# Filler matmuls in the idle stretches of a planned attention and MoE kernel, with a plan tuned anew

## The chip, the cores and the metric

The kernel runs on one core of one Trainium2 chip. The metric is the device time of one execution in microseconds (us); the number compared is the median of several runs. The engines are PE (matrix products), DVE (vector), ACT (scalar functions), POOL (the general-purpose engine) and SP, which issues most transfers.

## What is computed

Attention keeps only the 32 largest scores of each row, and its output feeds a two-layer network with the gate h * tanh(softplus(h)). Everything is float32 in effect; the two weight matrices arrive as float64.

```python
q, k, v: (4, 8, 576, 64)          # batch, heads, sequence, head width
w_in: (512, 2048), w_out: (2048, 512)
scores = q @ k.T / sqrt(64)
kth = the 32nd largest score of each row
attn = softmax(where(scores >= kth, scores, -1e9))
x = (attn @ v) as (2304, 512)     # the 8 heads side by side
h = x @ w_in
sp = where(h > 20, h, log1p(exp(min(h, 20))))
out = (h * tanh(sp)) @ w_out      # (2304, 512)
```

## The kernel before, in words

**A planner writes the order.** The kernel does not issue its work in loops. `build` describes every operation to a `Plan`: its engine, an estimated duration, what it depends on, which ring buffers it takes and frees, and a priority. `Plan.schedule` then plays the work through: again and again it takes, over all engines, the operation that could start earliest by its estimates, and at equal starts the one with the smaller priority number. The resulting start times fix the order of the instructions on each engine's queue; on the chip each queue runs in order and waits by semaphores. So durations and priorities change nothing that is computed, only the order. Some operations name a second way on another engine (`also`); the planner takes the way that ends first, with a penalty for the second way (BIAS).

**Attention.** A unit is one batch, one pair of heads and one tile of 128 query rows (the last tile of a sequence has 64 rows and both heads share one slot). A full unit has two slots, one per head; there are 144 slots. Per slot: PE transposes the queries and multiplies them with the keys (line 638), ACT copies the 576 scores out of PSUM (line 655), DVE finds the 24 largest (lines 670 to 684: eight maxima of eight chunks, then maxima and replacements). How many scores lie below the 24th largest is counted either by DVE (line 703) or by ACT with a sign function (line 699): the share CSH decides. POOL multiplies the mask into the scores (line 707), DVE takes the next eight maxima (line 713), which yields the threshold. The exponential and the masking are then done by ACT and DVE (lines 756 and 758) or, for a share MSH, by ACT and POOL (lines 748 to 752). PE transposes the weights (line 803), ACT copies them (line 809), PE multiplies them with the values (line 839), and DVE writes the normalized rows to xr (lines 855 and 858).

**Weights.** Both matrices are loaded in 16 pieces each of 512 KB (line 422) into staging buffers (pools STG and STX), and float64 is turned into float32 by bit operations: POOL shifts the low word (line 428), ACT scales the high word into PSUM (line 435), DVE joins them (line 445). The sign is put in by DVE (line 441) or, for a share SGN ("apart"), by an ACT sign pass (line 439) and a POOL product (line 450). Except for the first six pieces of the second matrix, each piece is split into a high and a low part for the matrix engine; the low part is a subtraction on POOL (line 476) or, for a share PLO, an identity product and a subtracting product on PE (lines 469 and 470) with a copy on ACT (line 473). While pieces are being prepared, six of the eight hidden-layer buffers serve as staging; `release` gives them back when the last piece is done.

**The network.** The 2304 tokens form 9 groups of 256. A group can start when all eight heads of its tokens are in xr; it is split into high and low parts (lines 906 to 917). The first layer is 16 blocks of 12 matmuls (line 940), the nonlinearity runs on ACT in batches (lines 952 to 972), POOL or DVE multiply and split (lines 987 to 1000), and the second layer accumulates 16 blocks in the two banks psO (lines 1009 and 1013) until `flush` copies them out and stores them. The planner's pool "O" has one entry: it is taken by a group's first block of the second layer and given back by the flush.

**Priorities.** Attention work has the slot's number plus an offset OFF[0..8, 11..] by kind (OFF[0] for loads of keys and queries, one less than that or more by a few), weight pieces WPR[0] + WPR[1] * i (+ WPO for the second matrix), group g of the network MLP0 + MLPS * 16 * g + LAG[g].

**The matrix engine's clock in the plan.** The planner counts the columns that PE streams in steps of TICK us; if the step before an operation had fewer than WARM, it plans the operation at twice its duration.

The planner's durations for DVE are linear in the length: `dve(n)` is (1.0417 n + 72) ns, `held(n, extra)` the same plus extra, for operations that exclude POOL in the plan.

Of the kernel before, what the change touches and what calls it, by code (L numbers as in the profile page):

```python
# [33 lines left out]
             TB=2, HB=8, GH=2, GL=3, XS=1, OB=1, C=2)  # L34
FIFO = ("S", "Y", "C", "M8", "SM", "WT", "WX", "RB", "KN", "KS", "QN", "QS", "QL", "V")
XR = 512
MLP0 = 58.83975636082121
MLPS = 1.121860262315038
LAG = (-25.995810819941177, -26.474079155792758, -19.13806320546605, -18.854128398230255, -7.786063767408372, -8.799346239468274, -12.371711128172647, -1.6692882578445132, -7.591562462708602)
OFF = (-16.98515120479643, 2.328093500794843, -3.96944656014681, 3.035426527996102, 0.4828418529158596, 0.7164642923464081, -1.649352757422735, 0.6592529327519733, -28.765739384772523, -3.5228328815861154, 6.763792071250068, -2.9083787972029063, 9.183328578610238)  # L40
WPO = -0.6274142379880567
CSH = [(18, 0.8667247802625605), (999, 0.3323003066774938)]
MSH = [(11, 0.919392917195224), (999, 0.13298644690001551)]
WPR = (19.149617763081373, 0.047652472774268644)
DELTA = 0
ALSO = True
N2 = 6
LOCK = True
TAB = 1.4
BIAS = [(48.89001834786856, 12.94226098178285), (724.1096866960131, 0.9005748864757063), (1000000000.0, 0.29275323803529374)]  # L50
PLO = [(16, 0.7434170351780047), (999, 0.21870871979825823)]
SGN = 0.3679529210622342
PH = {3: ([0, 1], [2], [3, 4])}

SLACK = {'pe': 0.2487527268649277, 'dve': 0.0, 'act': 0.0, 'pool': 0.3014222492564422}
TICK = 3.413
WARM = 3060

# [24 lines left out]
class Plan:  # L85
# [7 lines left out]
    def __init__(self, sizes):  # L93
        self.sizes = sizes
        self.ops = []
        self.slot = {}

    def op(self, eng, dur, fn, deps=(), alloc=(), free=(), prio=0.0, cols=0, also=(), tab=None):

# [8 lines left out]
    def schedule(self):  # L108
        free = {p: [(0.0, i) for i in range(n)] for p, n in self.sizes.items()}
        turn = {p: [] for p in FIFO}  # L110
        for o in self.ops:
            o.left = len(o.deps)
            for d in o.deps:
                d.users.append(o)
            for p in {p for p, _ in o.alloc}:
                if p in turn:
                    turn[p].append(o)
        for p in turn:
            turn[p].reverse()
        avail = {e: 0.6 if e == "sp" else 2.3 for o in self.ops for e, _, _ in o.ways}  # L120
        moved = 0.0
        port = {"pool": 0.0, "dve": 0.0}
        cand = [(o, [0.0] * len(o.ways)) for o in self.ops if o.left == 0]
        ndone = 0
        order = []
        ticks = {}

        loaded, window, left = "exp", None, 0

        def pool_ready(o):  # L130
            need = {}
            for p, _ in o.alloc:
                need[p] = need.get(p, 0) + 1
                if p in turn and turn[p][-1] is not o:
                    return None
            r = 0.0
            for p, n in need.items():
                if len(free[p]) < n:
                    return None
                r = max(r, sorted(free[p])[n - 1][0])  # L140
            return r

        while ndone < len(self.ops):
            best = {}
            for c in cand:
                o, rs = c
                if o.tab and window and (o.tab == "exp" or o.tab[1] != window):
                    continue
                pr = pool_ready(o) if o.alloc else 0.0
                if pr is None:  # L150
                    continue
                w = None
                for x, (e, d, _) in enumerate(o.ways):
                    load = TAB if o.tab and (o.tab == "exp") != (loaded == "exp") else 0.0
                    st = max(avail[e] + load, rs[x], pr)
                    if LOCK and e == "pool":
                        st = max(st, port["dve"])
                    elif LOCK and isinstance(d, Held):
                        st = max(st, port["pool"])
                    fin = st + d + (next(b for t, b in BIAS if st < t) if x else 0.0)  # L160
                    if w is None or fin < w[0]:
                        w = (fin, st, x)
                e = o.ways[w[2]][0]
                best.setdefault(e, []).append((w[1], o.prio, o.seq, w[2], c))
            if not best:
                stuck = sorted({(o.prio, o.eng, tuple(p for p, _ in o.alloc)) for o, _ in cand})
                raise RuntimeError(f"no operation can go on: {stuck[:12]}")
            pick = None
            for e, lst in best.items():
                lo = min(x[0] for x in lst) + DELTA  # L170
                x = min((y for y in lst if y[0] <= lo), key=lambda y: (y[1], y[2]) if DELTA else (y[0], y[1], y[2]))
                if pick is None or x[:3] < pick[:3]:
                    pick = x
            s, _, _, x, c = pick
            o = c[0]
            cand.remove(c)
            o.eng, o.dur, o.fn = o.ways[x]
            dur = o.dur
            if o.tab:
                loaded = o.tab if o.tab == "exp" else "trig"  # L180
                if loaded == "trig":
                    if window is None:
                        window, left = o.tab[1:]
                    left -= 1
                    if not left:
                        window = None
            if o.eng == "pe":
                tick = int(s / TICK)
                if ticks.get(tick - 1, 0) < WARM:
                    dur *= 2  # L190
                m = max(1, int(dur / 0.2))
                for i in range(m):
                    tk = int((s + dur * (i + 0.5) / m) / TICK)
                    ticks[tk] = ticks.get(tk, 0) + o.cols / m
            o.start = s
            if o.eng == "sp":
                avail["sp"] = s + o.cols
                moved = max(s + 1.2 * o.dur, moved) + o.dur
                o.end = max(moved, s + o.cols) + 1.25
            else:  # L200
                o.end = avail[o.eng] = s + dur
                if isinstance(o.dur, Sent):
                    o.end += Sent.LAND
                if o.eng == "pool" or isinstance(o.dur, Held):
                    port[o.eng] = o.end
            for p in {p for p, _ in o.alloc}:
                if p in turn:
                    turn[p].pop()
            for p, k in o.alloc:
                free[p].sort()  # L210
                t, i = free[p].pop(0)
                self.slot[k] = i
            for p, k in o.free:
                free[p].append((o.end + 0.2, self.slot[k]))
            for u in o.users:
                u.left -= 1
                if u.left == 0:
                    cand.append((u, [max(d.end + self.hop(d.eng, e) for d in u.deps) for e, _, _ in u.ways]))
            ndone += 1
            order.append(o)  # L220
        order.sort(key=lambda o: (o.start, o.seq))
        return order
# [35 lines left out]
def attn_moe_kernel(  # L258
# [9 lines left out]
    nc = tc.nc  # L268
# [88 lines left out]
    def build(fast, weights):  # L357
# [7 lines left out]
        order = []  # L365
# [214 lines left out]
        def unit(b, p, t, pkey, kready, vready, last, pr, final):  # L580
# [80 lines left out]
            if fast:  # L661
# [16 lines left out]
                for r in range(3):  # L678
                    for n in range(nt):
                        cur[n] = P.op("dve", dve(64), lambda n=n, r=r: nc.vector.max(M8()[:, n, r, :], Ct(n)),  # L680
                                      [cur[n]], free=[("C", ck[n])] if r == 2 else (), prio=pr + 0.2 + OFF[3])
                    if r < 2:
                        for n in range(nt):
                            cur[n] = P.op("dve", dve(64), lambda n=n, r=r: nc.vector.match_replace(
                                Ct(n), M8()[:, n, r, :], Ct(n), NEG), [cur[n]], prio=pr + 0.2 + OFF[3])
                nm = P.op("pool", 0.16, lambda: nc.gpsimd.tensor_scalar(
                    SM()[:, 0, 0:nt], M8()[:, 0:nt, 0, 0], -scale, 0.0, op0=ALU.mult, op1=ALU.add),
# [55 lines left out]
            for n in range(nt):  # L743
                if fast and share(MSH, n0 + n + 7):
# [10 lines left out]
                    continue  # L755
                e = P.op("act", acts(S, 1), lambda n=n: nc.scalar.activation(  # L756
                    Yt(n), St(n), AF.Exp, scale=scale, bias=SM()[:, 0, n:n + 1]), [nm, ym[n]], prio=pr + 0.6 + OFF[6], tab="exp")
                mk.append(P.op("dve", held(S, 60), lambda n=n: nc.vector.scalar_tensor_tensor(  # L758
                    Yt(n), St(n), th(n), Yt(n), op0=ALU.is_ge, op1=ALU.mult,
                    accum_out=SM()[:, 2, n:n + 1]), [e, kt[n]], free=[("S", Sk[n])], prio=pr + 0.7 + OFF[6]))  # L760

# [323 lines left out]

    def program(fast, weights):
        P = build(fast, weights)
        for o in P.schedule():
            o.fn()
        return P  # L1090
# [53 lines left out]
```

## Time and profile before

| what | value |
|---|---|
| median of 3 runs | 872.06 us (871.81 to 873.59) |
| the profiled execution's own time | 873.14 us |
| its span, first to last instruction | 871.3 us |
| mean granted clock of PE | 0.969 of full speed |
| busy share of PE, DVE, ACT, POOL | 93%, 78%, 76%, 65% |

The profile is one execution as the hardware profiler took it. Its span is a little shorter than the execution's time. Matmuls are pipelined and their ends are modelled, so a busy PE is not PE at its peak. "Idle before, releaser" names what ended an engine's wait, and the chain of waits is followed back from the last instruction of a stretch, at each step to what released it.

### The profile page before, as it was taken

The numbers are of one execution on the slowest core, as the hardware profiler recorded it, in microseconds if no ns is written. First come the engines' busy times: TensorE is split into PE (matmuls) and PEld (weight loads), VectorE is DVE, ScalarE is ACT, GpSimd is POOL, SyncE is SP. The second block draws the span as 40 slices with busy tenths as digits, with TensorE's granted clock in tenths as the row PEclk, the third lists the DMA queues.
The fourth block names the chain that finished last, engine by engine and source line by source line (L and its number), as shares of the span: only waits on it lengthen the run. The fifth ranks groups of instructions, "written<-read, shape, count | busy, mean of one in ns | idle before, by whom it ended". The sixth has DMA issues, their size and how long they took to land.

```text
span 871.3 us, 18564 instructions
## 1 busy us (share of the span) xinstructions
PE 811.7 (93%) x5752; PEld 603.1 (69%) x5752; DVE 680.6 (78%) x3265; ACT 657.9 (76%) x1398; POOL 568.0 (65%) x885
## 2 busy tenths in 40 slices
PE   5778697998999999999999999999999999999995
PEld 2445474575786687857776787777877788697964
DVE  5889999798998988988689989679978979502422
ACT  5868879688787786878978887897798797455840
POOL 4987878988967678567785795779687776100000
PEclk9677999999999999999999999999999999999998
DMA  6434334341111110202021102111111201000011
GB/s 159 114 104 127 119 93 123 106 113 37 34 32 50 39 33 18 64 21 49 20 57 39 23 25 51 47 25 35 38 51 42 60 21 39 14 26 1 1 25 29
DMA packets 87661, 45.81 MB, mean 53 GB/s; under 512 B 64768, under 2 KB 85504, under 8 KB 87552
## 3 DMA queue, kind: packets, MB, share of 16 engines
q1 hardware_dynamic: 86368, 43.87, 19.2%
q8 instruction: 48, 0.79, 0.4%
q10 hardware_dynamic: 1184, 0.66, 0.3%
q14 instruction: 61, 0.50, 0.2%
HBM read 39.78 MB, written 4.72 MB: 51 GB/s over the span
## 4 chain that ended last, share of the span: by engine, by line
PE 71%; POOL 11%; DVE 9%; ACT 5%; issue 2%; DMA 2%; SPq 0%; DVEq 0%; POOLq 0%; ACTq 0%
PE psH L940 17%; PE psO L1013 14%; PE psO L1009 9%; PE psW L638 9%; PE psW L839 8%; PE psW L803 6%; POOL Y L707 3%; PE psW L940 3%; DVE C L670 2%; DVE Y L758 2%; DVE M L713 1%; PE psW L545 1%; PE psW L612 1%; POOL mb L428 1%; PE psW L817 1%
## 5 line engine op out<-in xcount | busy, mean ns | idle before, releaser
L707 POOL TENSOR_TENSOR Y<-Y,S 128x576 f32<-128x576 f32 x137 | 193.5, 1421 | 0.1
L670 DVE MAX8 C<-S 128x8 f32<-128x72 f32 x1152 | 175.7, 219 | 14.1 <-ACT S L655 13.5
L940 PE MATMUL psH<-xh,wih 128*128 128x256 f32 x512 | 151.3, 295 | 0.0
L940 PE MATMUL psH<-xh,wil 128*128 128x256 f32 x512 | 143.0, 279 | 0.0
L940 PE MATMUL psH<-xl,wih 128*128 128x256 f32 x512 | 142.9, 279 | 0.0
L758 DVE SCALAR_TENSOR_TENSOR Y<-S,M,Y 128x576 f32<-128x576 f32 x121 | 111.6, 936 | 30.2 <-ACT Y L756 29.9
L655 ACT COPY S<-psW 128x288 f32<-128x288 f32 x288 | 102.7, 407 | 35.8 <-PE psW L638 34.2
L713 DVE MAX8 M<-Y 128x8 f32<-128x585 f32 x144 | 109.4, 760 | 18.6 <-POOL Y L707 17.7
L638 PE MATMUL psW<-KS,QS 64*128 64x288 f32 x512 | 105.1, 477 | 10.1 <-DVE mb L445 3.8
L756 ACT ACTIVATE Y<-S,SM 128x576 f32<-128x576 f32 x121 | 92.9, 780 | 22.6 <-DVE M L713 20.8
L803 PE MATMUL psW<-ident,Y 128*128 128x128 f32 (+1 forms) x640 | 88.1, 277 | 17.1 <-ACT Y L752 4.8
L940 PEld LDWEIGHTS psH<-xh,wih 128*128 128x128 f32 x512 | 96.2, 188 | 9.2 <-issue 6.3
L803 PEld LDWEIGHTS psW<-ident,Y 128*128 128x128 f32 (+1 forms) x640 | 67.4, 144 | 48.5 <-issue 12.3
L1009 PE MATMUL psO<-wof,mb 128*128 128x512 f32 x208 | 99.7, 609 | 0.8 <-POOL mb L987 0.8
L940 PEld LDWEIGHTS psH<-xl,wih 128*128 128x128 f32 x512 | 96.2, 188 | 0.5
L940 PEld LDWEIGHTS psH<-xh,wil 128*128 128x128 f32 x512 | 96.1, 188 | 0.0
L839 PEld LDWEIGHTS psW<-WT,V 128*64 128x64 f32 x1280 | 66.8, 142 | 33.6 <-ACT WX L825 8.7
L839 PE MATMUL psW<-WT,V 128*64 128x128 f32 (+1 forms) x1280 | 85.1, 277 | 3.4 <-ACT WX L825 3.4
L809 ACT COPY WT<-psW 128x512 f32<-128x512 f32 (+1 forms) x154 | 80.5, 549 | 7.3 <-PE psW L803 6.1
L680 DVE MAX8 M<-C 128x8 f32<-128x64 f32 x432 | 82.1, 215 | 1.1
L1013 PE MATMUL psO<-woh,GH 128*128 128x512 f32 x180 | 76.0, 422 | 0.0
L703 DVE TENSOR_SCALAR_CACHE_REDUCE Y<-S,M 128x576 f32<-128x576 f32 x87 | 69.7, 804 | 5.5 <-PE psW L819 3.2
(149 smaller groups left out, 1802.0 us busy)
## 6 DMA issues: line engine op xcount, KB each, us to landing
mb<-in_moe_w_in_dram SPq DMA_DIRECT2D x16, 512.0 KB, 4.0
mb<-in_moe_w_out_dram SPq DMA_DIRECT2D x16, 512.0 KB, 3.5
V<-in_v_dram SPq DMA_DIRECT2D x30, 256.0 KB, 2.8
QN<-in_q_dram SPq DMA_DIRECT2D x64, 64.0 KB, 2.0
KN<-in_k_dram SPq DMA_DIRECT2D x31, 128.0 KB, 2.7
KN<-in_k_dram SPq DMA_DIRECT2D x61, 64.0 KB, 2.6
out_dram<-OB SPq DMA_DIRECT2D x15, 128.0 KB, 2.0
out_dram<-OB SPq DMA_DIRECT2D x22, 64.0 KB, 2.1
```

Of the source, the lines that this page charges most:

```text
L638: nc.tensor.matmul(psW[P.slot[wks[n]]][:, 0:HS], g_(qpool, qs)[hp, :], KSt()[hp, rng], start=True, stop=True)
L655: return lambda: eng(St(n)[:, rng], psW[P.slot[w]][:, 0:HS])
L670: nc.vector.max(Ct(n)[:, j, :], St(n)[:, j * CW:(j + 1) * CW])
L707: y = either(pool2(S), held(S), lambda eng, n=n: eng.tensor_tensor(Yt(n), Yt(n), St(n), op=ALU.mult), [c], prio=pr + 0.5 + OFF[5])
L713: ym.append(P.op("dve", dve(S + PAD), lambda n=n: nc.vector.max(M8()[:, n, 3, :], Yw(n)), [y, x], prio=pr + 0.6 + OFF[6]))
L756: e = P.op("act", acts(S, 1), lambda n=n: nc.scalar.activation(Yt(n), St(n), AF.Exp, scale=scale, bias=SM()[:, 0, n:n + 1]), [nm, ym[n]], ...
L758: mk.append(P.op("dve", held(S, 60), lambda n=n: nc.vector.scalar_tensor_tensor(Yt(n), St(n), th(n), Yt(n), op0=ALU.is_ge, op1=ALU.mult, a ...
L803: nc.tensor.transpose(psW[P.slot[wk]][:, t_ * w:(t_ + 1) * w], Yt(n)[hp, c_:c_ + 128], ident[hp, hp])
L839: nc.tensor.matmul(psX[64 * h:64 * h + 64, 0:n_], lw, rhs, start=t_ == 0, stop=t_ == T)
L940: nc.tensor.matmul(w, a, b_, start=n == 0, stop=n == len(mm) - 1)
L1009: nc.tensor.matmul(psO[t], hb_()[:, e, ts_], wof[:, f, :], start=f == 0, stop=f == NF - 1)
L1013: nc.tensor.matmul(psO[t], c[:, ts_], y[:, f - N2, :], start=f == 0 and n == 0, stop=f == NF - 1 and n == 2)
```

## The change

New numbers for most priorities and shares; two durations of DVE in the plan; and fillers: where the plan leaves PE idle for more than 0.5 us and the psO banks are free, it puts matmuls of the identity with itself into 70% of that time, planned at 0.22 us each (0.44 at half clock), which write 128 columns of a psO bank that nobody reads. They count as columns for the planned clock.

```diff
-MLP0 = 58.83975636082121
-MLPS = 1.121860262315038
-LAG = (-25.995810819941177, -26.474079155792758, -19.13806320546605, -18.854128398230255, -7.786063767408372, -8.799346239468274, -12.371711128172647, -1.6692882578445132, -7.591562462708602)
-OFF = (-16.98515120479643, 2.328093500794843, -3.96944656014681, 3.035426527996102, 0.4828418529158596, 0.7164642923464081, -1.649352757422735, 0.6592529327519733, -28.765739384772523, -3.5228328815861154, 6.763792071250068, -2.9083787972029063, 9.183328578610238)
-WPO = -0.6274142379880567
-CSH = [(18, 0.8667247802625605), (999, 0.3323003066774938)]
-MSH = [(11, 0.919392917195224), (999, 0.13298644690001551)]
-WPR = (19.149617763081373, 0.047652472774268644)
+MLP0 = 59.054782250573986
+MLPS = 1.0954921829722524
+LAG = (-25.995810819941177, -31.152146332737303, -22.215463354061715, -8.808118521994201, -11.32125493754739, -9.968969691480831, -13.761980037187891, -10.757969747616325, -16.8152201088914)
+OFF = (-3.9674718150461334, 2.789916747474043, -2.69084326238363, 1.3234374990135198, -0.31592645588424667, 0.7164642923464081, -1.649352757422735, 0.6592529327519733, -30.29022323989321, -3.5414633854427198, 3.9434639094286053, -2.9083787972029063, 8.027472388677591)
+WPO = 7.334362729915607
+CSH = [(22, 0.7381150632227842), (999, 0.36798294093955136)]
+MSH = [(11, 0.9056363652872507), (999, 0.13298644690001551)]
+WPR = (27.407999257653035, 0.05995130710075151)
...
-BIAS = [(48.89001834786856, 12.94226098178285), (724.1096866960131, 0.9005748864757063), (1000000000.0, 0.29275323803529374)]
-PLO = [(16, 0.7434170351780047), (999, 0.21870871979825823)]
-SGN = 0.3679529210622342
+BIAS = [(48.89001834786856, 12.468513877743371), (715.8379192325722, 0.9005748864757063), (1000000000.0, -0.018424251991158713)]
+PLO = [(16, 0.7434170351780047), (999, 0.11277534611467173)]
+SGN = 0.050121457328979165
...
+FILL = (0.5, 0.7)
+FILLER = 0.22
...
+            gap = s - avail["pe"]
+            if o.eng == "pe" and self.filler and gap > FILL[0] and free["O"] and free["O"][0][0] <= avail["pe"]:
+                tick = int(avail["pe"] / TICK)
+                one = FILLER * (2 if ticks.get(tick - 1, 0) < WARM else 1)
+                m = int(gap * FILL[1] / one)
+                if m:
+                    x = Op([("pe", FILLER * m, lambda m=m: self.filler(m))], [], [], [], 0.0, o.seq - 0.5, 512 * m, None)
+                    x.start, x.end = avail["pe"], avail["pe"] + one * m
+                    for i in range(m):
+                        tk = int((x.start + one * (i + 0.5)) / TICK)
+                        ticks[tk] = ticks.get(tk, 0) + 512
+                    order.append(x)
...
-                            cur[n] = P.op("dve", dve(64), lambda n=n, r=r: nc.vector.match_replace(
+                            cur[n] = P.op("dve", 0.19, lambda n=n, r=r: nc.vector.match_replace(
...
-                mk.append(P.op("dve", held(S, 60), lambda n=n: nc.vector.scalar_tensor_tensor(
+                mk.append(P.op("dve", held(S, 110), lambda n=n: nc.vector.scalar_tensor_tensor(
...
+        if fast:
+            def filler(m):
+                for _ in range(m):
+                    nc.tensor.matmul(psO[1][:, 0:128], ident, ident, start=True, stop=True)
+
+            P.filler = filler
```

The shares work out as follows. The function `share(part, n)` says yes for item n when n + 1 times the share passes a whole number that n times it did not. Signs apart: 11 of 32 pieces before, 1 after. Low parts by PE: 13 of the 26 pieces that have one before, 12 after. Counts by ACT: 57 of 144 slots before, 60 after; of the first 36 slots 21 both times. Masks by POOL: 23 of 144 before, 22 after; the one that falls away is slot 3.

## Rows read from the trace of the kernel before

**Rows 1.** Part 1 of the page: busy time of each engine.
```profile
PE 811.7 (93%) x5752; PEld 603.1 (69%) x5752; DVE 680.6 (78%) x3265; ACT 657.9 (76%) x1398; POOL 568.0 (65%) x885
```

**Rows 2.** Stretches: length, busy us (x) PE PEld DVE ACT POOL, PEclk, DMA, GB/s.
```profile
0.00:230.00 230.00, 182.38 (x1164) 121.21 (x1165) 196.61 (x940) 179.47 (x400) 189.12 (x296) 0.90 0.38 105
...
28.00:60.00 32.00, 24.97 (x123) 15.12 (x121) 25.38 (x114) 24.93 (x59) 28.12 (x51) 0.57 0.34 95
...
75.00:88.00 13.00, 10.64 (x48) 6.62 (x48) 12.39 (x55) 10.15 (x25) 10.21 (x16) 0.61 0.37 111
...
20.00:140.00 120.00, 94.60 (x602) 62.19 (x602) 110.34 (x530) 99.66 (x233) 100.67 (x167) 0.84 0.41 116
...
204.00:230.00 26.00, 21.03 (x150) 14.79 (x147) 21.86 (x122) 19.40 (x40) 23.11 (x35) 0.93 0.12 28
...
230.00:861.60 631.60, 629.20 (x4591) 481.92 (x4589) 483.15 (x2323) 478.43 (x998) 378.92 (x590) 1.00 0.14 33
...
861.60:871.30 9.70, 0.08 (x2) 0.00 (x0) 0.81 (x3) 0.00 (x0) 0.00 (x0) 0.68 0.29 64
```

**Rows 3.** Waits (total, times, longest): PE after 230, SP, DVE 20-230.
```profile
PE psW L612 <- DMA QN<-in_q_dram: 0.4, 1, 0.4
...
SPq L605 <- PE psW L612: 177.1, 52, 14.0
...
DVE M L713 <- POOL Y L707: 9.4, 12, 2.2
```

**Rows 4.** Chain of waits by line: 28-60, 75-88, 88-110 and 110-230 us.
```profile
by line: POOL Y L707 25.8%; POOL Y L710 7.4%; POOL Y L750 7.4%; issue 7.1%; PE psW L469 6.4%; PE psW L839 5.4%; PE psW L638 4.9%; POOL RB L773 4.2%; POOL mb L428 4.1%; POOL wil L476 3.9%; POOL mb L450 3.2%; POOL klog L716 2.9%; ACT Y L752 2
...
by line: POOL Y L707 26.0%; PE psW L839 18.8%; POOL mb L428 14.2%; issue 9.0%; POOL Y L710 8.0%; POOL wof L450 7.7%; POOL RB L773 6.9%; POOL xl L911 5.7%; PE psW L817 3.4%; ACT WX L825 2.9%; PE psW L819 1.8%
...
by line: DVE C L670 12.2%; issue 10.0%; ACT psW L435 7.2%; DVE C L684 7.1%; DVE M L680 6.6%; ACT S L655 6.5%; POOL Y L707 6.3%; ACT WT L809 6.2%; ACT Y L699 6.1%; ACT Y L756 5.7%; DVE M L713 3.5%; ACT Y L752 3.5%; POOL xl L911 3.4%; DVE Y L
...
by line: issue 8.8%; POOL Y L707 8.0%; DVE C L670 7.2%; DVE M L713 6.4%; POOL wol L476 5.4%; DVE Y L758 5.1%; POOL mb L987 4.3%; POOL mb L428 4.2%; DVE mb L441 3.8%; DVE mb L445 3.5%; PE psW L803 3.1%; DVE Y L703 3.0%; DVE M L680 3.0%; DVE 
```

**Rows 5.** Its pieces, 110-230 us: first and last of 61 POOL, 94 DVE.
```profile
140.62 0.34 POOL Y L710
...
217.20 2.77 POOL Y L707 x2
...
109.98 0.20 DVE C L684
...
219.99 0.78 DVE M L713
```

**Rows 6.** Groups by line and form: count, busy us, mean ns, idle before.
```profile
L450 POOL TENSOR_TENSOR mb<-mb 128x512 f32<-128x512 f32 x8 | 8.8, 1097 | 1.1 <-DVE mb L445 1.0
...
L441 DVE SCALAR_TENSOR_TENSOR mb<-psW,mb 128x512 int32<-128x512 int32 x21 | 14.4, 686 | 10.0 <-POOL mb L428 9.9
...
L439 ACT ACTIVATE mb<-mb 128x512 f32<-128x512 f32 x11 | 7.5, 685 | 0.1
...
L469 PE MATMUL psW<-mb,ident 128*128 128x512 f32 x26 | 15.4, 674 | 3.8 <-POOL blog L696 1.0 <-ACT WT L809 1.0 <-POOL wih L461 1.0
...
L758 DVE SCALAR_TENSOR_TENSOR Y<-S,M,Y 128x576 f32<-128x576 f32 x121 | 111.6, 936 | 30.2 <-ACT Y L756 29.9
...
L684 DVE MATCH_REPLACE8 C<-M,C 128x64 f32<-128x64 f32 x288 | 58.8, 209 | 0.0
```

**Rows 7.** Line 476: instructions, ns min/median/max, first and last start.
```profile
L476 POOL TENSOR_TENSOR wol<-mb,woh x8: 1298/1314/1317, 127.0 to 203.4; 128x512 fp32r<-128x512 f32 x8
```

**Rows 8.** PE in order of time: first and last idle stretch of 21.
```profile
4.93 0.45 PE L612 MATMUL psW<-ident,QN 128*128 128x128 f32 x1 [4.93 <-DMA QN<-in_q_dram]
...
141.30 1.22 PE L638 MATMUL psW<-KS,QS 64*128 64x288 f32 x2 [2.25 <-DVE mb L445]
```

**Rows 9.** Stretches of PE alone: length, busy (x), PEclk, DMA, GB/s.
```profile
34.00:37.40 3.40, 3.40 (x24) 0.50 0.10 24
...
57.80:61.20 3.40, 3.40 (x31) 0.75 0.36 124
```

More of the change, by code (lines that the diff above doesn't have):

```diff
@@ L96, in __init__ @@
         self.slot = {}
+        self.filler = None
     def op(self, eng, dur, fn, deps=(), alloc=(), free=(), prio=0.0, cols=0, also=(), tab=None):
```

## The prediction, made before the result was known

> **What bounds the kernel now.** First the busy table: PE is busy for 93% of the span [rows 1], but a share over the whole span hides where the other 7% lies. So next the table of stretches [rows 2]. From 230 to 861.6 us PE is busy for 629.2 of 631.6 us at a granted clock of 1.00; the only DMA it waits for there costs it 0.4 us once [rows 3]. That part is fixed by PE's work alone. Before 230 us PE is busy for 182.4 of 230 us, so 47.6 us are idle, at a mean clock of 0.90. After 861.6 us come 9.7 us of copies and stores. Nothing in the middle can be won except by doing less on PE; what the change can move lies before 230 us, where the attention of the first tokens and the preparation of the weights have to be finished before PE has enough to do.
>
> Who sets the pace there is read from the chain of waits by stretch [rows 4]. From 28 to 60 us the named POOL lines are 58.9% of the chain, PE lines 16.7%; from 75 to 88 us POOL 68.5%, PE 24.1%. From 88 to 110 us DVE lines (29%) and ACT lines (35%) take over, and from 110 to 230 us POOL and DVE share it: 61 POOL pieces sum to 44.8 us, 94 DVE pieces to 44.0 us [rows 5], 37% each of 120 us. The longest wait of DVE from 20 to 230 us agrees: 9.4 us for POOL's product of line 707 [rows 3].
>
> **The sum is made against the profiled execution**, 873.14 us with a span of 871.3 us (1.84 us around it); that is 1.08 us above the median of the runs, 872.06.
>
> **Signs apart (SGN).** The share falls from 0.368 to 0.050: of 32 weight pieces, 11 took the way over ACT and POOL, now 1. Ten pieces lose one POOL product of 1.10 us (line 450) and one ACT pass of 7.5/11 = 0.68 us (line 439), and gain one DVE pass of 0.69 us (line 441) [rows 6]. POOL loses 11.0 us, ACT 6.8, DVE gains 6.9; half of it lies in the first weight matrix, before 110 us, half behind. I weigh each by its engine's share of the chain. POOL: 5.5 x 0.6 + 5.5 x 0.37 = **-5.3 us**. DVE: 3.4 x 0.06 (29% of 22 us, over 110 us) + 3.4 x 0.37 = **+1.5 us**. ACT: 3.4 x 0.07 before, nothing behind, where ACT is named in no leading line: **-0.2 us**. Ends: -11 us if POOL carried the chain alone, +6.9 us if DVE did.
>
> **Low parts (PLO).** 12 pieces instead of 13 get their low part from PE. PE loses three 512-column matmuls of 15.4/26 = 0.59 us [rows 6], 1.8 us, in a stretch where PE is hardly on the chain: nothing. POOL gains one subtraction of 1.31 us [rows 7], x 0.37: **+0.5 us**.
>
> **Counts and masks (CSH, MSH).** In the 36 slots before 230 us the counts on ACT stay 21 of 36 and only change places; behind, 3 more counts move from DVE to ACT, under PE's full stretch: nothing. Slot 3 is masked by DVE (111.6/121 = 0.92 us) instead of POOL, whose product (line 750) is 7.4% of 32 us for two, 1.2 us each, on the chain [rows 4, 6]; x 0.6: **-0.7 us**, DVE's part being off the chain there.
>
> **Fillers.** Before 142 us PE has 21 idle stretches over 0.5 us, 32.1 us together, the first and last shown [rows 8]. The planner puts fillers into 70% of a planned gap at 0.22 or 0.44 us each: some 51 to 102 of them, if its gaps are like the real ones. Nearest real operation: a plain 512-column f32 matmul, 0.59 us at mixed clock [rows 6], a quarter of that for 128 columns: 0.15 us, at half clock about 0.3. So they really take 8 to 31 us, the last only if all were slow; likelier is 15 us, half of the gaps, with the other half left as margin. Cost: nothing, hidden by the waits that make the gaps; without that cover, each late filler is 0.3 us at most, 21 times, 6 us. They can only be placed while the output bank is free, so hardly beyond group 0's second layer. Gain: the clock is 0.57 from 28 to 60 us and 0.61 from 75 to 88 us [rows 2]. PE on the chain is 16.7% of 32 us and 24.1% of 13 us [rows 4], 5.3 and 3.1 us; at full clock 43% and 39% of that would go, 3.5 us. Ends 0 and 3.5. I take two thirds, **-2.3 us**, because a busy PE alone does not lift the clock here: from 34.0 to 37.4 us PE was busy throughout at 0.50, with attention products and transposes, and only from 57.8 to 61.2 us, behind plain 512-column matmuls, did it come back in part, 0.75 [rows 9]. The fillers are plain full-array matmuls, but occupy only half of each gap.
>
> By the Trainium skill (TensorE: Matmul & The Clock Gate, Part 1) the gate follows how busy the engine has been lately, and activity lifts the throttle; by that the whole 3.5 us would be won. The row from 34.0 us does not agree with it: fully busy, still at 0.50.
>
> **Order.** New LAG, OFF, WPR, WPO change only which operation goes first among those that could start together. Key and query loads lose 13 places of lead on SP (OFF[0]), weight loads 8, second-matrix loads 16. SP's longest waits, 177 us, are for PE to free the one query buffer [rows 3]: a load goes out when its buffer frees, whatever its priority, so nothing; without that cover the one load that PE did wait for cost 4.9 us [rows 8]. The plan's DVE durations come nearer: replacement was planned at 0.139 us, now 0.19, and takes (58.8/288) 0.20; the masking was planned at 0.73, now 0.78, and takes 0.92 [rows 6]. A plan that knows this puts DVE's work in an order that waits less. Ends: the 9.4 us that DVE waits for POOL, won at most; on the other side the last rival below. I take nothing, as no row shows the new order.
>
> **Sum:** -5.3 + 1.5 - 0.2 + 0.5 - 0.7 - 2.3 = -6.5 us: 866.6 beside the profiled execution, 872.06 - 6.5 = 865.5 beside the median.
>
> **The rivals.**
> *Fillers that warm nothing* (0.09). The change then does not do what it says; the rest stays: 865.5 + 2.3 = 867.8 us. For it: the row from 34.0 us. Against: the return after 57.8 us.
>
> *DVE takes POOL's place* (0.12). DVE is busy for 110.3 of 120 us from 20 to 140 us [rows 2]. With 3.4 us more it has little slack, and POOL's relief of 6.0 us (5.3 and 0.7) stays without effect: 871.5 us, within 0.2%, which is about what a measurement of this kernel tells from no change. Against: its own waits are for POOL.
>
> *The order wins too* (0.14). All of DVE's 9.4 us for POOL goes: 856.1 us. For it: durations nearer the rows. Against: two engines near saturation leave little to reorder.
>
> *The second weight matrix comes too late* (0.21, slower). Its pieces lose 16 slots of priority (WPR +8.3, WPO +8.0). Its last subtraction on POOL starts at 203.4 us now [rows 7]; only then do staging buffers become hidden-layer buffers, and the second layer of group 0 needs those weights. From 204 to 230 us PE still does 21.0 of 26 us [rows 2]. If the pieces move back by that stretch's length, I put half of that work, 10.5 us, behind 230 us, where PE has no room: 865.5 + 10.5 = 876.0 us. It decides once the last subtraction is some 16 us (6.5/10.5 x 26) later than 203.4. For it: the shift is larger than any other priority's. Against: priority decides only among operations that are ready, and each piece waits for its buffer first.
>
> **How the numbers follow.** The sum itself holds 0.44. Faster by over 0.2%: 0.44 + 0.09 + 0.14 = 0.67; the same: 0.12; slower: 0.21. The likeliest case gives 865.5 us, on its own 857 (POOL's 12.2 us whole, fillers 3.5) to 870 (fillers nothing, half of POOL's). The range reaches to the order's win with some of POOL's ends, 853, and just past the slower rival, 877; outside lies about 0.15.
>
> **What would show it.** Right: the stretch from 230 us on still full at clock 1.00; the point from which PE is full some 6 us earlier; line 441 at 31 instructions, lines 439 and 450 at 1; POOL's share of the chain before 88 us smaller; the clock from 28 to 88 us well above 0.6; a new group of 50 to 100 filler matmuls on psO, none on the chain. Wrong: PE idle behind 230 us; a last subtraction of line 476 past 220 us; fillers on the chain; DVE leading the chain before 88 us.

## The result, and the profile after

| kernel | median us | runs | ratio to its own runs of before (95%) |
|---|---|---|---|
| before | 872.43 | 4 | 1 |
| after | 864.10 (862.29 to 865.29) | 4 | 0.9901 [0.9881, 0.9922] |

The change makes the kernel faster by 8.3 us; forecast were 865.5 us and -6.5. The profiled execution took 862.29 us with a span of 860.2, the shortest of the four: differences against its trace overstate by up to 1.8 us. Line numbers are those of after, some 15 higher than before.

The page of after: busy time by engine, and the granted clock in 40 slices (before [rows 1]).
```profile
PE 819.8 (95%) x5949; PEld 616.7 (72%) x5949; DVE 687.4 (80%) x3271; ACT 655.3 (76%) x1393; POOL 554.7 (64%) x875
...
PEclk9999999998999999999999999999999999999998
```
Stretches of after, with the columns of [rows 2]:
```profile
0.00:230.00 230.00, 200.18 (x1435) 145.46 (x1436) 203.41 (x960) 179.64 (x404) 177.14 (x282) 0.98 0.37 105
28.00:60.00 32.00, 27.69 (x205) 19.92 (x206) 28.73 (x131) 24.54 (x59) 27.13 (x48) 1.00 0.45 121
75.00:88.00 13.00, 11.66 (x100) 9.19 (x100) 12.95 (x59) 10.28 (x25) 11.00 (x20) 1.00 0.28 71
...
190.00:230.00 40.00, 31.49 (x212) 22.63 (x211) 32.91 (x149) 27.23 (x59) 36.22 (x53) 0.91 0.27 81
...
230.00:850.40 620.40, 618.70 (x4512) 470.81 (x4512) 482.99 (x2310) 474.93 (x989) 377.60 (x594) 1.00 0.14 34
```
The clock from 28 to 60 us rises from 0.57 to 1.00, from 75 to 88 us from 0.61 to 1.00. From 230 us on PE is as full as before, with 10.5 us less to do (618.7 against 629.2): that work now lies ahead of 230 us.

The groups of the fillers, of the sign pass that was added on DVE, and of the subtraction for the low part (this last with its first and last start):
```profile
L1107 PE MATMUL psO<-ident 128*128 128x128 f32 x200 | 30.9, 292 | 1.4 <-POOL ident masks.py:199 1.4
L457 DVE SCALAR_TENSOR_TENSOR mb<-psW,mb 128x512 int32<-128x512 int32 x31 | 21.2, 685 | 9.0 <-POOL mb L444 8.2 <-ACT psW L451 0.5
```
```profile
L492 POOL TENSOR_TENSOR wol<-mb,woh x9: 1286/1313/1844, 161.4 to 229.9; 128x512 fp32r<-128x512 f32 x9
```
The plan put in 100 fillers, each issued as two instructions, 30.9 us together. That is twice the 15 us that the prediction held likelier: it took one instruction for each. PE's books: without them it is busy for 788.9 us (811.7 before: -22.8); idle time and fillers together are 40.4 + 30.9 = 71.3 us (59.6 before: +11.7). The span is 11.1 us shorter. Less time on the same products (warm clock, one low part fewer) pays for more waiting.

The chain of waits of after by line, 75 to 88, 88 to 110 and 110 to 230 us (before [rows 4]):
```profile
by line: DVE C L686 24.0%; DVE M L729 16.5%; DVE mb L457 13.7%; DVE Y L774 11.3%; DVE mb L461 9.1%; DVE M L696 6.9%; DVE C L700 6.0%; DVE Y L719 5.6%; DVE xr L874 3.7%; DVE Y L726 1.7%; DVE SM L780 0.9%; issue 0.8%; DVE SM L781 0.3%
...
by line: PE psH L956 20.2%; PE psW L485 13.5%; PE psW L654 6.7%; POOL Y L723 6.3%; DVE C L686 6.1%; PE psW L855 5.7%; POOL Y L766 5.5%; PE psW L819 4.0%; ACT Y L768 4.0%; ACT Y L764 3.6%; ACT Y L715 3.5%; POOL SM L761 3.5%; DVE M L729 3.2%;
...
by line: PE psH L956 17.5%; PE psO L1025 9.1%; PE psW L654 8.3%; PE psW L855 8.1%; PE psO L1029 5.9%; issue 5.6%; POOL Y L723 4.6%; PE psW L819 3.9%; POOL wol L492 3.7%; DMA QN<-in_q_dram 2.7%; DVE M L729 2.5%; POOL mb L1003 2.1%; POOL Y L7
```
This view matters most. Before, POOL held 68.5% from 75 to 88 us, and POOL and DVE shared the stretch from 110 us on. Now DVE holds all of 75 to 88 us (in e9 below, the same instructions up to 122 us, some two thirds), and the leading lines behind 88 us are PE's. Three pieces of that last chain, at their start and length:
```profile
133.00 1.31 PE psO L1107 x10
...
136.18 3.22 DMA QN<-in_q_dram
...
139.84 0.45 PE psO L1107 x4
```
Fillers are on the chain, and so is a query load.

### The profile page after: what moved, and what is told of

Same layout as the page of the kernel before. It is cut to its first block, busy times and chain, and to the rows that moved or that the text cites. A ratio compares the mean times of both kernels' runs of the same rounds, so it can differ in the third digit from the quotient of the medians.

```text
span 860.2 us, 18912 instructions
## 1 busy us (share of the span) xinstructions
PE 819.8 (95%) x5949; PEld 616.7 (72%) x5949; DVE 687.4 (80%) x3271; ACT 655.3 (76%) x1393; POOL 554.7 (64%) x875
## 4 chain that ended last, share of the span: by engine, by line
PE 77%; DVE 8%; POOL 6%; ACT 5%; DMA 2%; issue 2%; ACTq 0%; POOLq 0%; DVEq 0%
PE psH L956 20%; PE psO L1029 14%; PE psO L1025 11%; PE psW L654 10%; PE psW L855 9%; PE psW L819 6%; PE psW L956 3%; POOL Y L723 2%; DVE C L686 2%; DVE Y L774 1%; DVE M L729 1%; PE psW L628 1%; PE psW L561 1%; PE psW L833 1%; DMA QN<-in_q_dram 1%
## 5 line engine op out<-in xcount | busy, mean ns | idle before, releaser
L723 POOL TENSOR_TENSOR Y<-Y,S 128x576 f32<-128x576 f32 x130 | 183.8, 1421 | 0.0
L772 ACT ACTIVATE Y<-S,SM 128x576 f32<-128x576 f32 x122 | 93.4, 780 | 24.5 <-DVE M L729 21.8
L654 PE MATMUL psW<-KS,QS 64*128 64x288 f32 x512 | 100.9, 458 | 1.0 <-ACT QS L641 0.4
L1025 PE MATMUL psO<-wof,mb 128*128 128x512 f32 x200 | 94.2, 601 | 0.0
L819 PE MATMUL psW<-ident,Y 128*128 128x128 f32 (+1 forms) x640 | 84.0, 272 | 5.5 <-ACT WT L825 1.1
L819 PEld LDWEIGHTS psW<-ident,Y 128*128 128x128 f32 (+1 forms) x640 | 64.2, 141 | 32.8 <-issue 10.0
L855 PEld LDWEIGHTS psW<-WT,V 128*64 128x64 f32 x1280 | 63.3, 137 | 27.8 <-issue 7.9
L855 PE MATMUL psW<-WT,V 128*64 128x128 f32 (+1 forms) x1280 | 81.0, 269 | 1.8 <-ACT WX L841 1.7
L1029 PE MATMUL psO<-woh,GL 128*128 128x512 f32 x180 | 72.1, 401 | 4.9 <-POOL GL L1016 4.9
```

Source lines behind the costliest of these rows:

```text
L654: nc.tensor.matmul(psW[P.slot[wks[n]]][:, 0:HS], g_(qpool, qs)[hp, :], KSt()[hp, rng], start=True, stop=True)
L723: y = either(pool2(S), held(S), lambda eng, n=n: eng.tensor_tensor(Yt(n), Yt(n), St(n), op=ALU.mult), [c], prio=pr + 0.5 + OFF[5])
L819: nc.tensor.transpose(psW[P.slot[wk]][:, t_ * w:(t_ + 1) * w], Yt(n)[hp, c_:c_ + 128], ident[hp, hp])
L855: nc.tensor.matmul(psX[64 * h:64 * h + 64, 0:n_], lw, rhs, start=t_ == 0, stop=t_ == T)
L1025: nc.tensor.matmul(psO[t], hb_()[:, e, ts_], wof[:, f, :], start=f == 0, stop=f == NF - 1)
L1029: nc.tensor.matmul(psO[t], c[:, ts_], y[:, f - N2, :], start=f == 0 and n == 0, stop=f == NF - 1 and n == 2)
```

## The experiments

The question is which part brought the 8.3 us. Theories: signs (the forecast's largest term), fillers, the order. The plan makes a second question: undoing a part lets the planner draw a new order. So there are two kinds of run, *planned again*, and *in a fixed order*, where the plan stays and only what its entries issue is changed. "Lag" compares the n-th copy on ACT of the attention output (line 841) in two traces.

| run | median us (runs) | ratio to before (95%) |
|---|---|---|
| e1_order_no_filler | 871.64 (10) | 1.0011 [0.9993, 1.0030] |
| e2_before_filled | 872.07 (10) | 1.0002 [0.9989, 1.0014] |
| e3_sgn_back | 888.55 (4) | 1.0195 [1.0178, 1.0212] |
| e4_sgn_alone | 903.62 (4) | 1.0369 [1.0351, 1.0386] |
| e5_before_twice_filled | 873.10 (10) | 1.0012 [0.9997, 1.0027] |
| e6_sgn_same_order | 874.50 (10) | 1.0024 [1.0015, 1.0034] |
| e7_sgn_back_same_order | 875.74 (5) | 1.0039 [1.0025, 1.0054] |
| e8_mask_112 | 880.83 (4) | 1.0102 [1.0084, 1.0120] |
| e9_early_fillers | 868.01 (5) | 0.9949 [0.9934, 0.9964] |
| e10_twice_fillers | 869.82 (7) | 0.9963 [0.9948, 0.9979] |
| e11_plan_again | 862.38 (4) | 0.9882 [0.9868, 0.9897] |
| e12_early_halved | 867.84 (6) | 0.9940 [0.9922, 0.9958] |

### After's order without the fillers

```diff
-                for _ in range(m):
+                for _ in range(0):
```


> The order of the changed kernel, instruction for instruction, with the fillers planned but not issued: what the fillers do on the chip, and nothing else. As predicted (fillers worth 2.3 us, at most 3.5, because PE is on the chain for 8.4 us of the cold stretches): 864.1 + 2.3 = 866.4 us, at most 867.6, with the clock of 28 to 60 us near 0.6 again. Rival (the warm clock carries most of the gain, since the changed order is built on it): 869 us or more. Rival (a warm clock in stretches that POOL and DVE pace is worth nothing): 864 us.

Measured: 871.64 us, no change against before. Shares, priorities and order by themselves bring nothing; the fillers bring 7.5 us in that order (by the two ratios 1.1%, 9.6 us), as the rival from 869 us on had it. The trace is of the shortest of the ten runs, 868.11 us; its span is 5.7 us longer than after's. Stretches of this run:
```profile
28.00:60.00 32.00, 27.17 (x139) 15.18 (x136) 28.34 (x127) 23.44 (x58) 26.04 (x47) 0.74 0.42 117
...
75.00:88.00 13.00, 9.60 (x65) 6.89 (x65) 11.72 (x58) 10.18 (x27) 9.20 (x16) 0.77 0.35 105
110.00:152.00 42.00, 37.08 (x261) 27.45 (x260) 37.22 (x170) 35.19 (x76) 28.76 (x46) 0.88 0.28 86
```
The clock is 0.74, 0.77 and 0.88 where it is 1.00 with the fillers. The chain by line from 28 to 60 and from 88 to 110 us:
```profile
by line: PE psW L654 14.0%; PE psW L485 11.8%; issue 7.4%; PE psW L855 7.4%; PE psW L819 5.2%; ACT S L671 4.3%; POOL Y L723 4.3%; DVE mb L461 4.0%; POOL mb L444 3.4%; ACT Y L715 3.3%; PE psW L486 3.0%; DVE Y L774 2.8%; PE psW L561 2.8%; DVE
...
by line: PE psW L654 23.5%; PE psW L855 16.3%; PE psW L485 13.5%; PE psH L956 8.4%; POOL Y L723 6.3%; ACT S L671 6.0%; PE psW L819 5.9%; ACT Y L715 3.5%; ACT Y L768 3.5%; PE psW L486 3.2%; PE psW L833 2.5%; ACT WT L825 2.2%; POOL Y L726 1.5
```
Without the fillers PE's named lines hold 44% of the first stretch, where after's chain has no line of PE, and 73% of the second (50% in after). So this order, run cold, puts PE on the chain, which before's order did not from 88 to 110 us [rows 4]. Its lag behind after is 2.4 us at 75 us, 3.1 from 98 to 130, 4.9 at 148, between 3.7 and 6.1 from 206 to 224, and mostly 4.7 to 5.6 from there to 744: gained early, then kept. One step is the jump at 148 us. Attention's copies around it, after first, then this run:
```profile
130.26 0.35 ACT L841 COPY WX<-psW 128x256 f32<-128x256 f32 x1
147.99 0.37 ACT L841 COPY WX<-psW 128x256 f32<-128x256 f32 x1
```
```profile
133.35 0.35 ACT L841 COPY WX<-psW 128x256 f32<-128x256 f32 x1
152.87 0.37 ACT L841 COPY WX<-psW 128x256 f32<-128x256 f32 x1
```
Between the two copies twelve matmuls of the second layer stand in PE's queue. PE's timeline, after first, then this run:
```profile
140.26 5.42 PE L1025 MATMUL psO<-wof,mb 128*128 128x512 f32 x12
```
```profile
143.46 7.09 PE L1025 MATMUL psO<-wof,mb 128*128 128x512 f32 x12 [0.80 <-POOL mb L1003]
```
They take 7.09 us instead of 5.42, and attention's next transposes wait behind them.

### The fillers in before's order, once and twice

```diff
+FILL = (0.5, 0.7)
+FILLER = 0.22
...
+            gap = s - avail["pe"]
...
+                    x.start, x.end = avail["pe"], avail["pe"] + one * m
+                    order.append(x)
```
For the second run `range(m)` becomes `range(2 * m)`. The fillers are not counted in the planned clock, so the order of the rest stays: 51 fillers, then 102.

> The order of the kernel before, instruction for instruction, with fillers put into its planned gaps by the same rule, but not counted in the planned clock. As predicted: 872.4 - 2.3 = 870.1 us, at least 868.9, clock of 28 to 60 us at 0.9 or more. Rival (fillers carry most of the gain): 867 us or less. Rival (fillers do nothing, or stand in the way of late matmuls): 872 us or more.

> The order of the kernel before, with twice the fillers of the run that put them into its gaps (some 204 matmul instructions instead of 102, as many as the changed kernel has). The one filling left the clock of 28 to 60 us at 0.73 and the time at 872.1. Theory (the fillers' worth hangs on the order: in the order of before POOL and DVE hold the chain from 88 us on and what a warm clock wins is given back there): the clock of 28 to 110 us at 0.95 or more and still 871 to 873 us. Rival (there were too few fillers, a clock fully up is worth what the prediction said, 2.3 to 3.5 us, or more): 870 us or less.

Measured: 872.07 and 873.10 us, both no change. Their stretch from 28 to 60 us, once and twice filled, then the chain by line of the latter from 110 to 230 us:
```profile
28.00:60.00 32.00, 25.26 (x139) 15.85 (x139) 26.19 (x115) 24.98 (x61) 28.16 (x52) 0.73 0.33 96
```
```profile
28.00:60.00 32.00, 24.76 (x170) 17.46 (x169) 24.86 (x110) 24.43 (x60) 27.04 (x49) 0.89 0.35 97
```
```profile
by line: issue 8.8%; DVE C L683 8.5%; POOL Y L720 8.3%; DVE M L726 7.5%; DVE Y L771 5.8%; POOL wol L489 5.4%; POOL mb L1000 4.3%; POOL mb L441 4.2%; DVE mb L454 3.7%; DVE M L693 3.5%; DVE mb L458 3.5%; DVE C L697 3.5%; DVE Y L716 3.1%; PE p
```
Here the clock rose (0.89; 0.94 from 28 to 110 us, just short of the 0.95 expected; mean 0.986) and the time did not fall: the chain stays with DVE and POOL. In the once filled run attention is 2.6 us ahead of before at 83 us and 0.7 at 100: what was won is given back. In before's order a warmer PE is worth nothing; in after's 7.5 us. So neither the order nor the fillers bring anything alone; the 8.3 us come from both together.

### The signs, planned again

```diff
-SGN = 0.050121457328979165
+SGN = 0.3679529210622342
```
in after (e3), the reverse in before (e4).

> The changed kernel with the share of pieces whose sign is put in by ACT and POOL back at 0.368 (11 pieces instead of 1), planned anew with all else as in the changed kernel. As predicted (POOL's relief -5.3, DVE's load +1.5, ACT -0.2): 864.1 + 4.0 = 868.1 us. Rival (DVE leads the early chain now, so POOL's relief is worth nothing): 864 us or less.

> The kernel before with that share at 0.050 and nothing else changed, planned anew. As predicted: 872.4 - 4.0 = 868.4 us, with POOL's lines a smaller part of the chain before 88 us. Rival (the ten passes land on a full DVE): 872 us or more.

Measured: 888.55 and 903.62 us. Both directions are slower by far, which no price of the signs that is the same in both orders can do. The suspicion: every change of the plan's input draws another order, and both kernels' orders are better than a random draw. The test of that changes a planned duration by 2 ns, and nothing that a shared-out part does:

```diff
-                mk.append(P.op("dve", held(S, 110), lambda n=n: nc.vector.scalar_tensor_tensor(
+                mk.append(P.op("dve", held(S, 112), lambda n=n: nc.vector.scalar_tensor_tensor(
```


> The changed kernel with one planned duration moved by 2 ns (masking planned at 600 + 72 + 112 ns instead of 110), everything else as it is, planned anew: the same work, the same shares, another order. Theory (every new plan is a new draw of the order, so a part undone with a new plan measures the draw, not the part): away from 864 us by 5 us or more, as the two re-planned runs with another sign share were by 24 and 31 us. Rival (orders that follow from nearly the same durations take nearly the same time, and the two re-planned runs show what the sign share is worth): 862 to 866 us.

Measured: 880.83 us, 16.7 us behind after, by 2 ns in the plan. Its stretch from 230 us:
```profile
230.00:867.50 637.50, 631.29 (x4573) 483.09 (x4572) 485.53 (x2298) 469.59 (x978) 362.74 (x576) 1.00 0.13 32
```
PE idles 6.2 us here, 1.7 in after. The new plan also holds 111 fillers instead of 100. A new plan alone can thus cost as much as two thirds of e3's difference, 24.5 us: e3 and e4 cannot tell the share from the draw. All three redraws came out slower than the kernels that they started from, which fits the suspicion; three do not prove it.

### The signs in a fixed order

In before's order the ten pieces get their sign on DVE at the place of the join, and the ACT pass and POOL product fall away (e6); in after's order the reverse (e7).
```diff
-                        sg = P.op("act", acts(PN), lambda: nc.scalar.activation(word(1), word(1), AF.Sign), [x], prio=pr)
+                        sg = P.op("act", acts(PN), lambda: None if swap else nc.scalar.activation(word(1), word(1), AF.Sign), [x], prio=pr)
...
+                    def join():
+                        if swap:
+                            nc.vector.scalar_tensor_tensor(
+                                word(0, I32), high(), -2 ** 31, word(0, I32), op0=ALU.bitwise_and, op1=ALU.bitwise_or)
...
-                        o = P.op("pool", pool2(PN), lambda: nc.gpsimd.tensor_tensor(
+                        o = P.op("pool", pool2(PN), lambda: None if swap else nc.gpsimd.tensor_tensor(
```


> The order of the kernel before, with the ten sign pieces done in the new way inside it: ten ACT sign passes and ten POOL products left out, ten DVE passes put in front of the joining pass, nothing planned anew. As predicted (POOL -5.3, DVE +1.5, ACT -0.2): 872 - 4.0 = 868 us. Rival (the freed POOL time is not passed on, as DVE or the group that PE waits for is set elsewhere): 871 to 873 us. Rival (DVE's 6.9 us count in full): 876 us or more.

> The order of the changed kernel, fillers included, with the ten sign pieces done in the old way inside it: the sign pass on ACT behind the scaling pass, the product on POOL behind the joining pass, the DVE pass left out. If POOL's time is worth on this order what the prediction said: 864.1 + 4.0 = 868 us. Rival (this order keeps DVE on the chain from 75 to 88 us, POOL has room): 863 to 865 us, or faster by DVE's 6.9 us times its share.

Measured: 874.50 us (before on the same chip 872.00) and 875.74 us. Their first 230 us, e6 and then e7:
```profile
0.00:230.00 230.00, 185.28 (x1138) 121.78 (x1140) 198.63 (x939) 173.23 (x386) 175.91 (x284) 0.87 0.37 104
```
```profile
0.00:230.00 230.00, 194.46 (x1338) 138.19 (x1340) 189.15 (x903) 177.62 (x395) 178.02 (x274) 0.95 0.36 102
```
In e6 POOL is busy 13.2 us less than before (175.9 against 189.1) and the kernel is 2.5 us *slower*. POOL's freed time is not passed on: DVE, which got the ten passes, waits for POOL's product as long as before (9.4 us [rows 3]), from 20 to 230 us:
```profile
DVE M L723 <- POOL Y L717: 9.7, 8, 2.6
```
The lag is 0.1 us at 94 us, 2.8 at 193, and 2.4 to 2.8 to the end. In e7 the way back costs 11.6 us, in an order made for the new way, and DVE waits 13.6 us for POOL's line 445, the shift (8.2 in after). Neither is the price of the signs by itself: the old way fits the old order, the new way the new one.

### How many fillers

After's order each time: only those planned before 100 us (e9 leaves out 18 of 100), each twice (e10), the early ones halved (e12: 47 of 82, all 18 late).
```diff
+                    late = avail["pe"] > 100
...
+                    x = Op([("pe", FILLER * m, lambda m=0 if late else m: self.filler(m))], [], [], [], 0.0, o.seq - 0.5, 512 * m, None)
```
```diff
-                for _ in range(m):
+                for _ in range(2 * m):
```
```diff
+                    k = m if avail["pe"] > 100 else (m + 1) // 2
```


> The order of the changed kernel with the fillers planned before 100 us only: the 18 of 100 that stand behind (36 of 200 matmul instructions, 122 to 140 us) are left out. Without any filler the same order runs 7.5 us longer, and attention falls behind by 3.1 us up to 110 us and by 1.8 us more from 130 to 148 us. Theory (the late ones keep the clock up where layer 1 has put PE on the chain): 866 to 867 us, the clock of 110 to 152 us near 0.9. Rival (what counts is the clock up to 100 us, the later lag only follows from it): 863.5 to 865 us.

> The order of the changed kernel with every run of fillers twice as long (some 400 matmul instructions). The clock is 1.00 from 20 to 140 us already, so nothing is to be won but in the first 28 us (0.94). Theory (the fillers take only half of the gaps, the margin covers as many again): 863 to 866 us. Rival (late fillers hold up real matmuls; 62 us of fillers in some 70 us of idle and filler time leave no margin): 868 us or more.

> The order of the changed kernel with the fillers planned up to 100 us halved (47 instead of 82) and the later 18 whole. Theory (the early fillers are needed in full to keep the clock at 1.00, where a half filling left it at 0.73 in the order of before): 866 us or more, the clock of 28 to 60 us below 0.9. Rival (half is enough, and shorter runs hold up less): 862 to 864.5 us.

Measured: 868.01, 869.82 and 867.84 us. Without the 18 late fillers the time is 3.9 us longer by the medians, more than the 2 to 3 us expected; the twelve matmuls take 7.11 us again:
```profile
141.35 7.11 PE L1026 MATMUL psO<-wof,mb 128*128 128x512 f32 x12 [0.35 <-POOL mb L1004]
```
The traces show 1.7 us of the 3.9 there (the lag goes from 1.1 to 2.8 us at 148 us). The 1.1 us stand from 82 us on, ahead of the first filler that was left out, and 1.0 us comes behind 744 us; the late fillers do not explain these.

Twice as many lose 5.7 us against after. The stretches 28 to 60 and 60 to 75 us of that run:
```profile
28.00:60.00 32.00, 31.73 (x249) 25.05 (x247) 27.45 (x113) 22.73 (x54) 24.59 (x42) 1.00 0.35 99
60.00:75.00 15.00, 15.00 (x124) 11.81 (x124) 14.32 (x65) 13.68 (x31) 12.67 (x21) 1.00 0.46 122
```
PE has no gap left, at a clock that was full already; the lag is 3.5 us at 42 us and 5.5 from 148 us on. The fillers are then work ahead of attention's own.

The halved run was to lose by a colder clock. It does not: the stretch from 28 to 60 us reads 1.00.
```profile
28.00:60.00 32.00, 26.02 (x179) 16.90 (x179) 28.39 (x130) 24.92 (x61) 26.98 (x50) 1.00 0.47 125
```
Yet it is 3.7 us slower, and the two intervals only just touch, at 0.9922. In its one trace it is 1.9 us behind from 32 to 130 us, so the halved fillers in between cost nothing more; it is 3.2 behind at 148 us and 4.5 at 224. At the start POOL begins the shift of the third weight piece 1.05 us later than in after (12.66 against 11.61 us), but e11 below has most of that too (12.35) and is not slow. Why e12 is slower at a full clock stays open, and with it whether the clock is all that the early fillers give.

### Another plan

Priorities and shares moved a little to another plan by the planner's own estimate; a few of the numbers:
```diff
-WPO = 7.334362729915607
+WPO = 6.639056982790353
...
-BIAS = [(48.89001834786856, 12.468513877743371), (715.8379192325722, 0.9005748864757063), (1000000000.0, -0.018424251991158713)]
+BIAS = [(55.61094913281963, 11.824236470425335), (729.9657180458274, 0.9021212104914098), (1000000000.0, -2.7508851177855997)]
```


> The changed kernel with priorities and shares moved a little further, so that the same planner, fillers counted, ends a little earlier by its own count; nothing else. Theory (the plan's own end follows the chip closely enough to pick orders by): 861.5 to 864 us, at or below the changed kernel's 864.1. Rival (at this level the picked orders differ from their plans by several us): 866 us or more.

Measured: 862.38 us, 0.9882 [0.9868, 0.9897]. It lies 1.7 us below after's median, but the intervals overlap: not shown to be faster than after.

## Why the prediction was right, and where it was not

**The time** came out in the forecast's own case: -8.3 us where -6.5 stood, inside its range of 857 to 870. Its make-up was wrong, and errors of both signs cancelled: that the sum came so close is luck.

**Signs**, -4.0 us of the sum, the largest term: not confirmed. The counts came as worked out (line 457 at 31 instructions, one piece left on the old way), and POOL's busy time before 230 us fell by 12 us. In before's order that relief gave +2.5 us. The step that failed weighed each engine by its share of the chain *of the kernel before*, as if time taken from POOL shortened the chain by that share. In a fixed order it did not (e6); what it may give in a new order is in the bundle that e1 measures, which gave nothing. In that bundle the rival in which DVE takes POOL's place came true (871.5 us forecast, 871.64 measured, DVE leading from 75 to 88 us in after). The small terms, low parts and masks, were not tested by themselves.

**Fillers**, -2.3 us with ends 0 and 3.5: mis-sized by a factor of three, 7.5 us, past the upper end. The step that failed is the same: PE was given its chain share of before, 16.7% and 24.1%, and nothing behind 88 us. In the new order PE leads the chain behind 88 us, and run cold it leads from 28 to 60 us too (e1); the 18 late fillers alone are worth 1.7 us in the traces and 3.9 by the medians. Their cover was also wrong in part: some are on the chain, and twice as many cost 5.7 us.

**The clock.** The prediction took two thirds because of the row from 34.0 us, busy and still at 0.50. After's row of 28 to 60 us says 1.00: with fillers in the gaps the clock stays full. The row from 34.0 us was one busy stretch with idle time behind it (PE is busy for 1.1 of the next 3.4 us), and did not speak for an order whose gaps are filled.
The Trainium skill (TensorE: Matmul & The Clock Gate, Part 1) has it that activity releases the throttle; the rows of after agree (0.57 before, 1.00 after). By that reading the prediction had 3.5 us for the fillers, the nearer of its two figures, and still under half of what they brought.
That a clock nearly full need not shorten anything is e5's finding.

**Order**, 0 us with both ends open: e1's 871.64 us agrees, as the net of order and shares. The prediction's fillers-warm-nothing rival would then have been 871.6 and not 867.8 us. Of the DVE durations alone nothing can be said: every change of them draws a new order.

**Loads**, costed at nothing because they go out when a buffer frees: PE waited 4.3 us for query loads before 230 us, but 3.2 of it for the first load, for which before waits too (4.9 us). PE's wait for the first load, and for the one that is on the chain from 136.18 us:
```profile
5.79 0.47 PE L628 MATMUL psW<-ident,QN 128*128 128x128 f32 x1 [3.21 <-DMA QN<-in_q_dram]
...
139.54 0.30 PE L628 MATMUL psW<-ident,QN 128*128 128x128 f32 x1 [0.83 <-DMA QN<-in_q_dram]
```
The second left PE idle for 0.83 us, fillers having taken 1.60 us of the time that it was under way. So the term was not nothing; PE's waits put it at some 1 us, and what it is worth in time stays open.

**The slower rival** met its condition: the last subtraction starts at 229.9 us instead of 203.4, 26.5 us later, where 16 were to decide. The price was wrong: from 190 to 230 us PE did 2.5 us less than before (31.5 busy against 34.0), not 10.5. The same stretch in before:
```profile
190.00:230.00 40.00, 33.99 (x242) 24.33 (x242) 33.20 (x151) 29.82 (x62) 35.69 (x52) 0.96 0.22 60
```
That PE's warmer time ahead of it paid for this is likely, but not shown by itself.

**The signs of error** that the prediction named came true in three of four cases: the late subtraction, fillers on the chain, DVE leading from 75 to 88 us. The fourth decided: PE is not idle behind 230 us (618.7 of 620.4 us). The first reading, that the middle is fixed by PE's work and that all is decided before 230 us, held in each fixed-order comparison followed to the end: lags grow there and change by 1.2 us at most from 239 to 744 us, with up to 1.3 us more behind that. It is not a law of the kernel: e8, planned again, idled 6.2 us behind 230 us.

**Not settled:** why e12 is slow at a full clock, and how the 7.5 us of the fillers divide: 1.7 are seen at the twelve matmuls, the rest lies in a lag that grows from the start.

## What to carry to other kernels

An engine's share of the chain prices a saving only as long as the order stays and the chain with it: ask which engine leads the chain in the *new* order before weighing a term. Where a planner writes the order, undo a part with the order held fixed; a replanned ablation measures the draw as well (2 ns in one planned duration: 16.7 us). Even a fixed order favours the way that it was planned for: the signs lost in both directions, 2.5 and 11.6 us. Fillers for the clock pay where the matrix engine is on the chain behind the gap, and their number has a best value: 0, 100 and 200 gave 871.6, 864.1 and 869.8 us here.

## What the runs showed of the hardware that was not expected

After's order without fillers took 868.1 to 878.8 us in ten runs, and 862.3 to 865.3 in four with them. Low clock alone does not make such a scatter: before, with a mean clock of 0.969, took 870.8 to 873.8 us in nineteen runs beside them. What does stays open.

The granted clock from 28 to 60 us follows more than the number of fillers. In that stretch after has 64 filler instructions and e12 has 34, and both read 1.00; in before's order 10 left it at 0.73 (e2) and 39 at 0.89 (e5). So with 34 and 39 the two orders differ: by these traces, what stands between the fillers matters besides how many there are.
